# A new order for all operations of an attention and token-mixing kernel

## The chip, the cores and the metric

The kernel runs on one core of a Trainium2 chip. The metric is the device time of one launch in microseconds (us). A change of the order of operations is looked at, in a kernel whose order is written out by hand.

## The reference

For 8 batches and 8 heads, with q, k, v of 576 rows of 64 and p of 32 rows of 64:

```python
def sm_attn(qq, kk, vv):
    s = scale * np.matmul(qq, kk.transpose(0, 1, 3, 2))
    a = softmax(s)
    return np.matmul(a, vv)
p_packed = sm_attn(p, k, v)                # 32 packed rows per head
x = sm_attn(q, p_packed, p_packed)         # 576 rows per head
x = x.transpose(0, 2, 1, 3).reshape(8, 576, 512)
wq, wk = x @ w_q, x @ w_k                  # 576 x 64 each
W = (1/8) * wq @ wk.T                      # 576 x 576 per batch
out = np.maximum(W @ x, 0.0) @ w_out       # 8 x 576 x 512, float32
```

Inputs and output are float32.

## The kernel before

The text SCHEDULE holds 651 entries such as `oe2@2s` or `pv@6:4`: the name of an operation, its batch, the engine that does it (v for VectorE or DVE, s for ScalarE or ACT, g for GpSimd or POOL) or a form (A, C), and behind the colon the PSUM banks that it uses. The kernel issues them one after the other, so that each engine's queue, and each queue of transfers, has its entries in list order. Between engines only data and buffers hold an instruction back. An entry that has to wait holds up all that stands behind it in its own queue, and nothing else.

One batch goes through these operations; k and q lie in three thirds t, the output in four blocks c of 128 rows and a rest (c = 4) that two batches share:

- `LK`, `LQ`, `LV` load k, q, v of a batch (line 172, issued by POOL, with the cast to bf16). `LP`, `cw`, `wo` load p, w_q with w_k, and w_out in the same queue. The k of batch 0 comes as float32 (`k_f`, SP queue) and is cast by `cA`, `cB`.
- `kt`, `qt` turn the thirds on TensorE (PE, line 306); `ke`, `qe` bring them from PSUM to SBUF.
- `s0` (327) are the scores of p and k, `nm`, `ex` (337, 343) their softmax, `xt`, `xe` turn it; `rc1`, `mk` make the divisor.
- `pv` (389) multiplies with v, `pp` (403) divides; `pt`, `pte` turn the result; `pq`, `pqe` multiply it with w_q and w_k.
- `et`, `em` (439, 456) are the scores of q; `mx`, `sb`, `x`, `sm`, `rr`, `ml` (468 to 512) their softmax; `at`, `ae` turn it.
- `wk`, `wl`, `wq`, `g`, `y` and their evictions (`wke`, `wqe`, `ge`, `ye`), with `wkx` on POOL (582), make the factors of the token mixing; `m0`, `m1`, `m2` (648, 672) mix, `r00` to `r2` are the relu.
- `o0` to `o4` (691) are the projections with w_out, `oe0` to `oe4` evict them to o_sb0 (o0, o1), o_sb1 (o2, o3) and ox (o4).
- `st0`, `st1`, `st2` (711, 707) store o_sb0, o_sb1 and ox, all on the SP queue; in the last batch `sc0` to `sc3` (714) store single blocks.
- `u` is a matmul on zeros whose result nobody reads.

Buffers: SLOTS gives the number of buffers of each tile. k_sb, v_sb and q_sb have 6; o_sb0, o_sb1 and ox have 2. An eviction to o_sb0 of batch b therefore waits until the store of batch b - 2 has read that buffer, and likewise for o_sb1. PSUM has 8 banks; an operation that writes a bank waits for the eviction that last read it.

In form A an operation on PE uses the whole 128 columns of its weights, else two halves of 64; in form C a mix is cut into twice as many matmuls of 64 columns.

Of the kernel before, what the change touches and what calls it, by code (L numbers as in the profile page):

```python
# [7 lines left out]


SCHEDULE = """  # L10
    u@0:0 u@0:0 u@0:0 u@0:0 u@0:0 u@0:0 u@0:0 u@0:0 u@0:0 tp@0:3 cA0@0v cA1@0s cB0@0s kf1@0:7
    cB1@0v kf0@0:4 kf3@0:0 kfe3@0s kf2@0:1 LP@0 kfe1@0v lp@0v LQ@0 kfe2@0s kfe0@0v u@0:2 u@0:2
    s0@0:0 tr@0:43 nm0@0 u@0:5 u@0:5 u@0:5 qt1@0:7 nm1@0 ex0@0 LV@0 ex1@0 lq0@0v LK@1 LQ@1 u@0:5
    u@0:5 xt0@0:6 qt0@0:0 LK@2 qe1@0s cw0@0 xt1@0:7 xe0@0v qt2@0:1 rc1@0 xe1@0v mk@0 qe0@0s
    u@0:5 pv@0:5 pp0@0 u@0:2 pt@0:5 u@0:2 u@0:2 u@0:2 u@0:2 u@0:2 kt2@1:6 qe2@0s cw1@0 pte@0s
    cw2@0 et@0:0 em@0:A lq1@0s kt1@1:3 kt0@1:4 mx0@0 mx1@0 ke2@1s ke1@1v u@0:7 u@0:7 u@0:7
    qt0@1:3 sb1@0 ke0@1s cw3@0 s0@1:5 x1@0 qt1@1:4 sb0@0 u@0:0 u@0:0 u@0:0 u@0:0 kt2@2:0 kt0@2:1
# [35 lines left out]
    oe2@4v r10@5s r11@5s ml2@6g em@7 o0@5:1 pq@7:2 r2@5s mx0@7 at1@6:3 ae1@6s at0@6:4 o4@5:0
    ae0@6s mx1@7 wk@6:4 sb1@7 sb0@7 wl@6 x1@7 st0@4 wq@6:3 o3@5:5 wke@6s sm1@7v wkx@6g oe4@5v
    st2@3 x0@7 rr1@7v oe0@5s g@6:4 o2@5:6 sm0@7v ge@6s ml1@7g rr0@7v y@6:0 o1@5:7 ml2@7g ml0@7v
    oe3@5s oe2@5s pqe@7s wqe@6s at0@7:2 oe1@5s at1@7:6 ye@6v st1@4 m0@6:30C m1@6:15C ae0@7v
    ae1@7s wk@7:2 r00@6s r01@6v wl@7 wke@7s wq@7:6 r11@6v wkx@7g o1@6:7 g@7:0 o0@6:4 oe1@6s
    ge@7v y@7:2 r10@6s wqe@7v oe0@6s st1@5 ye@7v o3@6:0 st0@5 oe3@6v m2@7:1 m1@7:23 r2@7s r10@7s
# [11 lines left out]
def kernel(  # L70
# [308 lines left out]
    @op  # L379
    def pv(b, on, ks):  # L380
        if len(ks) == 1:
            ks = [ks[0], ks[0] + 1]
            S_[b]["pv"] = pair(ks[0], P)
        ps = [bank(kk, [P]) for kk in ks]
        for j in range(NJ):
            for gp in range(2):
                for h2 in range(2):
                    r = slice(64 * h2, 64 * h2 + 64)
                    nc.tensor.matmul(
                        ps[h2][64 * gp:64 * gp + 64], S_[b]["e1"][r, j, 64 * gp:64 * gp + 64],  # L390
                        S_[b]["v_sb"][r, gp::2, j, :], start=(j == 0), stop=(j == NJ - 1),
                    )
# [366 lines left out]
```

## Time and profile before

| | us |
|---|---|
| median of 3 runs | 123.13 (122.69 to 127.52) |
| profiled execution | 123.27 |
| its span, first to last instruction | 121.5 |
| PE busy | 105.8 (87%) |
| DVE busy | 91.3 (75%) |
| ACT busy | 80.5 (66%) |
| POOL busy | 56.3 (46%) |
| read from and written to HBM | 30.21 MB, 9.44 MB |

The table comes from the profile's page. Busy time of PE is that of pipelined matmuls, and 33 of them are the `u` on zeros (10.6 us). In a row of a group or of the timeline stands the line, the engine, what is written and read, the count and the time; "idle before" is how long the engine had nothing to run ahead of it, and what ended that. In the chain that ended last each step is followed back to what released it. The packets of the software queue, which carries the loads, take 72.3% of the span of the 16 transfer engines, those of the hardware queue of SP, which carries the stores and k_f, 23.3%.

### The profile page before, as it was taken

The page shows a single profiled execution, that of the slowest core. Times are in us where ns is not written, and L with a number is a line of the kernel's source. Part 1 is how long each engine was busy: PE and PEld are TensorE (multiplying, and loading weights), DVE is VectorE, ACT ScalarE, POOL GpSimd, SP SyncE. Part 2 cuts the span into 40 slices and gives each one's busy share as a digit, 9 for nine tenths or more (in the row PEclk, how much of TensorE's full clock was granted, in tenths as well). Part 3 has the DMA queues.
Part 4 walks back from the last instruction along what each step waited for, and adds up shares of the span by engine and source line. Part 5 has one row for each costly group of instructions (what it writes and reads, how often), then busy time and mean ns, then how long its engine had stood idle before and what let it go on. Part 6 is the DMA issues. An engine that isn't in the chain of part 4 may idle for free.

```text
span 121.5 us, 4739 instructions
## 1 busy us (share of the span) xinstructions
PE 105.8 (87%) x2051; PEld 70.9 (58%) x2060; DVE 91.3 (75%) x155; ACT 80.5 (66%) x176; POOL 56.3 (46%) x81
## 2 busy tenths in 40 slices
PE   6865788869998999999789999999799999999940
...
DMA  3999999999999999999999999999980037263692
GB/s 61 369 183 195 200 208 207 190 207 208 206 212 204 206 210 207 289 247 250 208 255 279 259 237 273 258 199 180 309 202 5 3 147 289 90 264 155 270 347 96
DMA packets 18069, 25.47 MB, mean 210 GB/s; under 512 B 2304, under 2 KB 14592, under 8 KB 18048
## 3 DMA queue, kind: packets, MB, share of 16 engines
q0 software_dynamic: 14064, 14.49, 72.3%
q1 hardware_dynamic: 3712, 10.62, 23.3%
q8 instruction: 16, 0.26, 0.8%
...
HBM read 30.21 MB, written 9.44 MB: 326 GB/s over the span
## 4 chain that ended last, share of the span: by engine, by line
DMA 42%; PE 30%; POOL 14%; ACT 5%; issue 4%; DVE 2%; ACTq 0%; POOLq 0%; DVEq 0%
DMA v_sb<-in_v_dram 20%; PE psum L691 14%; DMA k_sb<-in_k_dram 13%; DMA q_sb<-in_q_dram 9%; PE psum L155 3%; PE psum L306 3%; POOL q_sb L172 3%; POOL part_sum L492 3%; PE psum L648 2%; ACT o_sb L162 2%; POOL a L512 2%; POOL pT_bd L198 1%; POOL v_sb L172 1%; PE psum L456 1%; POOL k_sb L172 1%
## 5 line engine op out<-in xcount | busy, mean ns | idle before, releaser
L691 PE MATMUL psum<-w_out,reluT 128*64 128x512 bf16 (+1 forms) x196 | 31.5, 380 | 0.5 <-issue 0.2
L512 POOL TENSOR_TENSOR a<-e,rr 128x512 bf16<-128x512 f32 (+1 forms) x22 | 18.2, 853 | 12.4 <-DVE rr L501 6.3
L691 PEld LDWEIGHTS <-reluT 128*64 128x64 bf16 (+1 forms) x204 | 12.7, 106 | 9.5 <-ACT reluT L162 0.7
L468 DVE TENSOR_REDUCE mx<-psum 128x36 f32<-128x1152 f32 (+2 forms) x10 | 11.0, 1114 | 5.6 <-PE psum L456 5.1
L306 PE MATMUL psum<-ident,q_sb 128*64 128x128 bf16 x288 | 12.4, 220 | 3.1 <-DMA q_sb<-in_q_dram 2.4
L343 ACT ACTIVATE e1T<-psum,nmax 128x576 bf16<-128x576 f32 x16 | 11.7, 737 | 4.8 <-DVE nmax L337 4.6
L162 ACT ACTIVATE o_sb<-psum 128x512 f32<-128x512 f32 x19 | 11.4, 598 | 5.2 <-PE psum L691 4.5
L582 POOL TENSOR_TENSOR wkx<-wk,hmask 128x256 bf16<-128x256 bf16 x8 | 5.3, 668 | 20.0 <-ACT wk L162 15.7
L162 ACT ACTIVATE reluT<-psum 128x512 bf16<-128x512 f32 x22 | 12.3, 607 | 2.7 <-PE psum L648 2.7
L306 PEld LDWEIGHTS <-q_sb 128*64 128x64 bf16 x288 | 9.8, 109 | 5.2 <-DMA q_sb<-in_q_dram 3.8
L337 DVE TENSOR_REDUCE nmax<-psum 128x2 f32<-128x1152 f32 (+1 forms) x9 | 10.9, 1222 | 1.6 <-PE psum L327 1.5
L213 PE MATMUL psum<-blank 128*64 128x512 bf16 x33 | 10.6, 439 | 1.2 <-DVE blank L193 1.2
L480 ACT ACTIVATE e<-e 128x1152 f32<-128x1152 f32 (+2 forms) x10 | 9.7, 973 | 2.5 <-DVE e L472 1.8
L472 DVE TENSOR_TENSOR e<-psum,mx 128x1152 f32<-128x1152 f32 (+2 forms) x10 | 11.0, 1113 | 0.2
L358 POOL TENSOR_TENSOR mk<-mask,rrec 128x256 f32<-128x256 f32 x8 | 5.0, 621 | 13.0 <-DVE rrec L354 13.0
L306 PE MATMUL psum<-ident,k_sb 128*64 128x128 bf16 x252 | 10.3, 220 | 0.4 <-DMA k_sb<-in_k_dram 0.3
L168 DVE COPY o_sb<-psum 128x512 f32<-128x512 f32 x13 | 8.7, 683 | 2.3 <-PE psum L691 1.5
L486 DVE TENSOR_REDUCE rs<-e 128x36 f32<-128x1152 f32 (+2 forms) x9 | 9.6, 1075 | 0.5 <-ACT e L480 0.5
L306 PEld LDWEIGHTS <-k_sb 128*64 128x64 bf16 x252 | 8.3, 110 | 2.7 <-DMA k_sb<-in_k_dram 1.3
L162 ACT ACTIVATE qT<-psum 128x384 f32<-128x384 f32 x15 | 7.4, 498 | 1.7 <-PE psum L306 1.6
L162 ACT ACTIVATE a2T<-psum 128x320 f32<-128x320 f32 (+1 forms) x12 | 4.7, 418 | 4.3 <-PE psum L155 4.0
L162 ACT ACTIVATE kT<-psum 128x384 f32<-128x384 f32 (+2 forms) x14 | 6.3, 480 | 1.4 <-PE psum L306 1.2
...
## 6 DMA issues: line engine op xcount, KB each, us to landing
out_dram<-o_sb SPq DMA_DIRECT2D x14, 512.0 KB, 5.4
q_sb<-in_q_dram POOLq DMA_DIRECT2D x8, 576.0 KB, 13.2
v_sb<-in_v_dram POOLq DMA_DIRECT2D x8, 576.0 KB, 12.3
k_sb<-in_k_dram POOLq DMA_DIRECT2D x7, 576.0 KB, 16.3
k_f<-in_k_dram SPq DMA_DIRECT2D x2, 576.0 KB, 4.8
out_dram<-ox SPq DMA_DIRECT2D x4, 256.0 KB, 4.6
out_dram<-o_sb SPq DMA_DIRECT2D x4, 256.0 KB, 3.1
w_out<-in_moe_w_out_dram POOLq DMA_DIRECT2D x2, 256.0 KB, 9.7
```

Source lines behind the costliest of these rows:

```text
L162: nc.scalar.activation(dst, src, func, scale=scale)
L168: nc.vector.tensor_copy(dst, src)
L213: nc.tensor.matmul(bank(ks[0], [n])[0:64], blank[:, 0:64], blank[:, 0:n], start=True, stop=True)
L306: nc.tensor.transpose(ps[64 * g2:64 * g2 + 64, 2 * gp:2 * gp + 2, jj, :], S_[b][src][:, gp + 2 * g2, j], ident,)
L337: nc.vector.tensor_reduce(tile("nmax", [P, 2], fp32, b)[:, h], S_[b]["s1"][:, h], axis=AX, op=MAX, negate=True)
L343: nc.scalar.activation(tile("e1T", [P, NJ, 2, 64], bf16, b)[:, :, h2], S_[b]["s1"][:, h2].rearrange("a (j s) -> a j s", s=64), EXP, bias=S ...
L468: nc.vector.tensor_reduce(tile("mx", [P, NU, 1], fp32, b)[:, r], S_[b]["e"][:, r], axis=AX, op=MAX)
L472: nc.vector.tensor_tensor(tile("e2", [P, NU, L], fp32, b)[:, r], S_[b]["e"][:, r], S_[b]["mx"][:, r].to_broadcast((P, r.stop - r.start, L) ...
L480: nc.scalar.activation(e, e, EXP, scale=scale)
L486: nc.vector.tensor_reduce(dst, src, axis=AX, op=ADD)
L512: (nc.vector if on == "v" else nc.gpsimd).tensor_tensor(tile("a2", [P, NU, L], bf16, b)[:, r], S_[b]["e2"][:, r], S_[b]["rr"][:, r].to_bro ...
L691: nc.tensor.matmul(ps[r], src[:, h2, gp, o + r.start:o + r.stop], w_out[:, 2 * gp + h2, :], start=(h2 + gp == 0), stop=(h2 + gp == 2),)
```

## The change

The list is written anew: 655 entries in place of 651. Every operation of the old list is in the new one, and four `u` are added. The order differs nearly everywhere, some entries name another engine, another bank or another form, and `pv` can take a form E, which no entry uses. SLOTS and all else are the same. Of the list the rows that hold the loads and the stores of the first half, and the entries around them, are shown:

```diff
 SCHEDULE = """
-    u@0:0 u@0:0 u@0:0 u@0:0 u@0:0 u@0:0 u@0:0 u@0:0 u@0:0 tp@0:3 cA0@0v cA1@0s cB0@0s kf1@0:7
-    cB1@0v kf0@0:4 kf3@0:0 kfe3@0s kf2@0:1 LP@0 kfe1@0v lp@0v LQ@0 kfe2@0s kfe0@0v u@0:2 u@0:2
-    s0@0:0 tr@0:43 nm0@0 u@0:5 u@0:5 u@0:5 qt1@0:7 nm1@0 ex0@0 LV@0 ex1@0 lq0@0v LK@1 LQ@1 u@0:5
-    ...
-    LV@1 qe1@1s nm0@1 qt2@1:4 x0@0 ex1@1 sm0@0v kt1@2:2 LK@3 LQ@2 sm1@0v ex0@1 xt0@1:5 pq@0:7
-    ke2@2s rr0@0v ke0@2s wo1@0 ke1@2s rr1@0v xt1@1:0A ml1@0v ml0@0g ml2@0g qe2@1v pqe@0v at1@0:4
-    wo0@0 xe0@1s xe1@1v rc1@1 s0@2:5 LV@2 mk@1 at0@0:2 ae1@0s pv@1:0 ae0@0s LK@4 nm0@2 pp0@1
-    ...
-    o0@0:0A rr0@1v LQ@5 qe1@2s mk@2 LV@4 r11@0s nm0@3 ml0@1g ml1@1g ex1@3 r10@0v pv@2:2 o3@0:7A
-    ...
-    m1@1:70C pt@3:6A nm0@4 o1@1:5A qe2@3v pte@3s at1@2:6A LQ@6 ex0@4 r10@1v r11@1v o4@1:1A
-    ...
-    oe2@1s kt2@5:5 ge@2s ke0@5v sm0@3v y@2:0 rr0@3v pv@4:2 ye@2s m0@2:01C st0@0 pp0@4 r00@2v
-    ...
-    et@4:0 oe3@1s at1@3:5A st1@0 ml0@3g em@4:A qe2@5s o2@2:3A ae1@3s at0@3:5A oe2@2s o1@2:7A
-    mx0@4 ae0@3v wk@3:5A wl@3 wq@3:3 kt2@6:4 sb0@4 wqe@3v qt0@5:6 oe1@2s s0@5:0 pq@4:3 wke@3s
-    kt0@6:5 x0@4 qe0@5v pqe@4s ke2@6s nm0@5 qt1@5:6 wkx@3g kt1@6:7 ke0@6s sm0@4g ke1@6v st0@1
-    ...
-    xt1@5:7A rc1@5 oe0@2v kt2@7:5 rr0@4v r00@3s mk@5 ml1@4g xe0@5v kt0@7:6 r01@3s s0@6:0 xe1@5s
-    ...
-    ex1@6 pte@5s ml0@4g LV@6 st2@1 et@5:0 LQ@7 ml2@4g st1@1 ke1@7v oe2@3v o3@3:4A em@5:A qe2@6s
-    ...
-    o0@3:3A LV@7 r2@3s sb0@5 wl@4 rc1@6 mk@6 qt1@6:5 xe1@6s s0@7:0 wq@4:4 wke@4v oe0@3s wkx@4g
-    x0@5 nm0@7 pv@6:6 wqe@4s qe1@6s pp0@6 g@4:3A ge@4v o4@3:4A ex0@7 sm0@5v y@4:5 qt0@6:3
-    ...
-    ge@5s qe0@7v st0@2 y@5:0 pv@7:3 ye@5s st1@3 sm0@6v m0@5:67C pp0@7 m1@5:01C oe1@4s pq@6:5
-    ...
+    LP@0 LK@1 LQ@0 cA1@0s u@0:0 u@0:0 u@0:0 u@0:0 u@0:0 u@0:0 u@0:0 u@0:0 u@0:0 tp@0:0 LV@0 LK@2
+    cB0@0v cB1@0v LQ@1 cA0@0v u@0:1 u@0:1 u@0:1 u@0:1 u@0:1 u@0:1 u@0:1 kf3@0:4 cw3@0 kf0@0:5
+    kfe3@0v LV@1 lp@0v kf2@0:1 kfe0@0s kf1@0:4 kfe2@0s tr@0:26 kfe1@0v cw0@0 s0@0:3 nm0@0 ex0@0
+    ...
+    LK@3 pp0@0 pt@0:0A nm0@1 pte@0s u@0:2 et@0:0 em@0:A mx0@0 ex1@1 kt1@2:3 mx1@0 kt2@2:4 ex0@1
+    ...
+    u@0:0 at0@0:4 qe1@1v s0@2:0 ml2@0v LV@2 pv@1:5 ae0@0v pq@0:4 pp0@1 LK@4 at1@0:3A nm0@2
+    pt@1:5A wo1@0 pte@1s pqe@0s u@0:7 et@1:5 ae1@0s em@1:A wo0@0 ex0@2 wk@0:3A mx0@1 wl@0 wke@0s
+    ...
+    r01@0s u@0:2 pv@2:1 r11@0v ml2@1g qe0@2s ml0@1g qe2@2s s0@3:4 pp0@2 nm0@3 LV@4 u@0:3 at0@1:1
+    ...
+    sb0@3 qe0@4s wl@2 qt2@4:0 wke@2s kt2@5:7 pqe@3v kt1@5:6 wkx@2g x0@3 qe2@4v m0@1:12C LV@5
+    ...
+    qt0@5:3 pte@4v kt0@5:1 qe0@5s et@4:4 em@4:A ke0@5v qe1@5s oe2@1s at0@3:3A mx0@4 at1@3:0A
+    ae0@3s st1@1 m1@2:27C ae1@3s m0@2:13C r10@2s st0@0 o1@1:0A r11@2s sb0@4 r00@2s wk@3:2A
+    oe1@1s wl@3 wq@3:7 r01@2v x0@4 s0@5:4 wke@3v qt2@5:1 nm0@5 kt1@6:3 wqe@3s wkx@3g kt0@6:0
+    qe2@5s kt2@6:2 LQ@6 ke0@6s pq@4:7 kt2@7:1 ke1@6v ex0@5 kt1@7:0 LV@6 pqe@4v g@3:3A sm0@4v
+    ...
+    oe1@2s m1@3:34 LQ@7 xe1@5v s0@6:0 xe0@5v r10@3s o0@2:7 LV@7 r11@3s nm0@6 ml2@4g pv@5:3
+    oe0@2s ml0@4g m0@3:65 ex0@6 pp0@5 st0@2 kt0@7:7 pt@5:3 ml1@4g st2@1 ex1@6 o2@2:4 pte@5v
+    ke0@7v st1@0 r00@3s et@5:1 st0@1 qt0@6:0 r01@3s em@5:A qe0@6s xt1@6:5A mx0@5 xt0@6:6A xe1@6s
+    o3@2:0A xe0@6s at0@4:5A rc1@6 oe2@2s oe3@2v mk@6 qt2@6:6 o3@3:7 ae0@4s sb0@5 qe2@6s pv@6:4
+    ...
+    m2@3:4A sm0@5v wk@4:7A o2@3:3A ex1@7 r2@3s et@6:0 em@6 rr0@5v oe1@3s rc1@7 ml0@5g qt2@7:4
+    ...
+    pv@7:3 ye@4s rr0@6v ae0@5s m0@4:12 oe4@3s ml0@6g pp0@7 m1@4:75 wq@5:0 r01@4s st2@3 pt@7:3
+    ...
+    oe1@7s o2@7:0A sc1@7 oe0@7v o3@7:5A sc0@7 oe2@7v o4@7:4A sc2@7 oe3@7s sc3@7 oe4@7s st2@7
 """
 ...
@@ -107,8 +107,8 @@
     for item in SCHEDULE.split():
         name, rest = item.split("@")
         b, ks = rest.split(":") if ":" in rest else (rest, "")
-        on = ks[-1] if ks[-1:] in ("A", "C") else b[-1] if b[-1] in "vsg" else ""
-        items.append((name, int(b.rstrip("vsg")), on, [int(x) for x in ks.rstrip("AC")]))
+        on = ks[-1] if ks[-1:] in ("A", "C", "E") else b[-1] if b[-1] in "vsg" else ""
+        items.append((name, int(b.rstrip("vsg")), on, [int(x) for x in ks.rstrip("ACE")]))
     listed = {(name, b): on for name, b, on, _ in items}
 
     sbp = ctx.enter_context(tc.tile_pool(name="sbp", bufs=1))
@@ -381,6 +381,18 @@
         if len(ks) == 1:
             ks = [ks[0], ks[0] + 1]
             S_[b]["pv"] = pair(ks[0], P)
+        if on == "E":
+            ps = [bank(kk, [Dh]) for kk in ks]
+            S_[b]["pv"] = pair(ks[0], Dh).unsqueeze(2).to_broadcast((P, 2, 2, Dh))
+            for j in range(NJ):
+                for u in range(4):
+                    for h2 in range(2):
+                        r, c = slice(64 * h2, 64 * h2 + 64), slice(32 * u, 32 * u + 32)
+                        nc.tensor.matmul(
+                            ps[h2][c], S_[b]["e1"][r, j, c], S_[b]["v_sb"][r, u // 2 + 2 * (u % 2), j, :],
+                            start=(j == 0), stop=(j == NJ - 1),
+                        )
+            return
         ps = [bank(kk, [P]) for kk in ks]
         for j in range(NJ):
             for gp in range(2):
@@ -400,7 +412,10 @@
                 mask.rearrange("r g d -> r (g d)"), op0=MULT, op1=MULT,
             )
         else:
-            nc.vector.tensor_tensor(t, S_[b]["pv"], S_[b]["mk"], op=MULT)
+            m = S_[b]["mk"]
+            if len(S_[b]["pv"].shape) == 4:
+                t, m = (x.rearrange("r h (g d) -> r h g d", g=2) for x in (t, m))
+            nc.vector.tensor_tensor(t, S_[b]["pv"], m, op=MULT)
 
     for i in range(2):
         ops[f"pp{i}"] = lambda b, on, ks, i=i: pp(i, b)
```

More of the change, by code (lines that the diff above doesn't have):

```diff
@@ L53 @@
[L53 to L58, printed above, removed]
@@ L59 @@
-    m0@7:64 r00@7v st0@6 o2@6:5 r11@7s o3@7:1 oe2@6s r01@7v o4@7:5 o2@7:0 o0@7:3 st2@5 o1@7:4
-    st1@6 oe3@7v sc3@7 oe4@7s st2@7 oe2@7v oe0@7v sc2@7 oe1@7s sc0@7 sc1@7
+    LP@0 LK@1 LQ@0 cA1@0s u@0:0 u@0:0 u@0:0 u@0:0 u@0:0 u@0:0 u@0:0 u@0:0 u@0:0 tp@0:0 LV@0 LK@2
+    cB0@0v cB1@0v LQ@1 cA0@0v u@0:1 u@0:1 u@0:1 u@0:1 u@0:1 u@0:1 u@0:1 kf3@0:4 cw3@0 kf0@0:5
+    kfe3@0v LV@1 lp@0v kf2@0:1 kfe0@0s kf1@0:4 kfe2@0s tr@0:26 kfe1@0v cw0@0 s0@0:3 nm0@0 ex0@0
+    u@0:7 u@0:7 u@0:7 u@0:7 u@0:7 kt1@1:1 nm1@0 ex1@0 rc1@0 u@0:7 u@0:7 u@0:7 u@0:7 u@0:7
@@ new lines @@
+    pt@1:5A wo1@0 pte@1s pqe@0s u@0:7 et@1:5 ae1@0s em@1:A wo0@0 ex0@2 wk@0:3A mx0@1 wl@0 wke@0s
+    u@0:4 kt1@3:4 ex1@2 wkx@0g kt2@3:3 sb0@1 LQ@3 ke2@3s g@0:0 xt1@2:1A LV@3 ke1@3v xt0@2:2A
+    x0@1 wq@0:3 xe0@2v LQ@4 pq@1:5 rc1@2 xe1@2v qt0@2:4 ge@0s wqe@0s sm0@1v mk@2 y@0:6 qt2@2:0
+    ye@0s LK@5 kt0@3:3 pqe@1s qt1@2:1 ke0@3s rr0@1v m0@0:56C qe1@2v m1@0:37 ml1@1g r00@0s r10@0v
+    r01@0s u@0:2 pv@2:1 r11@0v ml2@1g qe0@2s ml0@1g qe2@2s s0@3:4 pp0@2 nm0@3 LV@4 u@0:3 at0@1:1
+    pt@2:2A ae0@1s at1@1:3A pte@2s ae1@1v et@2:0 ex1@3 em@2:A wk@1:3A LQ@5 ex0@3 mx0@2 wl@1
@@ new lines @@
+    wq@1:7 wke@1s kt1@4:4 pq@2:5 wkx@1g rc1@3 kt2@4:6 sb0@2 ke1@4s xt0@3:3 wqe@1s LK@6 o1@0:4A
+    xe0@3s LK@7 pqe@2v x0@2 xt1@3:0A g@1:5A mk@3 kt0@4:2 ge@1v xe1@3s o2@0:1 sm0@2v oe1@0s
+    ke0@4s qt1@3:4 ke2@4s y@1:2 qe1@3s rr0@2v s0@4:5 ye@1v ml0@2g qt2@3:4 nm0@4 o3@0:0 qe2@3s
+    ml2@2g qt0@3:4 ml1@2g oe3@0v ex1@4 pv@3:2 oe2@0s o0@0:0A pp0@3 ex0@4 at0@2:1A m2@1:2A qe0@3s
+    at1@2:3A oe0@0s r2@1v pt@3:5A xt0@4:4A ae0@2s pte@3v m1@1:67C ae1@2s rc1@4 qt1@4:0 r10@1s
+    mk@4 et@3:1 pq@3:5 qe1@4s em@3:A xe0@4s o4@1:0A r11@1s mx0@3 wk@2:6A oe4@1s qt0@4:7 wq@2:4
```

45 lines of the change are left out of this document (20 added, 25 removed).

## The prediction

> **What bounds the kernel now.** I read the page first, then the matrix engine's and the SP queue's timelines, the chain that ended last, and each transfer's time to landing.
>
> ```profile
> span 121.5 us, 4739 instructions
> PE 105.8 (87%) x2051; PEld 70.9 (58%) x2060; DVE 91.3 (75%) x155; ACT 80.5 (66%) x176; POOL 56.3 (46%) x81
> PE   6865788869998999999789999999799999999940
> DMA  3999999999999999999999999999980037263692
> ```
>
> The slices are 3.04 us long. Transfers fill the first 30 (91 us): the loads stream without a pause. PE is near full from slice 9 on. So two things run side by side, a load stream that ends at 91 us and a PE row that is dense from about 27 us to 117 us. PE's timeline shows how rarely loads still stop it late on, and the chain shows how it ends:
>
> ```profile
> 39.89 0.70 PE L389 MATMUL psum<-v_sb,e 64*64 64x128 bf16 x36
> 61.24 0.70 PE L389 MATMUL psum<-v_sb,e 64*64 64x128 bf16 x36 [1.26 <-DMA v_sb<-in_v_dram]
> 83.88 0.70 PE L389 MATMUL psum<-v_sb,e 64*64 64x128 bf16 x36
> 87.25 0.53 PE L306 MATMUL psum<-ident,q_sb 128*64 128x128 bf16 x12 [0.78 <-DMA q_sb<-in_q_dram]
> ...
> 111.32 5.33 PE psum L691 x48
> 116.66 0.02 issue
> ```
>
> L389 is operation pv: these are pv@2, pv@4 and pv@6. After pv@2 only pv@4 (1.26 us) and qt1@7 (0.78 us) wait for a load. From pv@2 to the last projection PE takes 116.66 - 39.89 = 76.8 us; from there to the end of the span lie 121.5 - 116.7 = 4.8 us (last eviction, last store). Outside the span lie 123.27 - 121.5 = 1.77 us of the profiled execution, which is 0.14 us above the median of the runs.
>
> **The change, part by part.** It adds a form of pv (letter E) that no entry of the new list uses: nothing. The list keeps every operation, adds four dummy matmuls u, and reorders the rest.
>
> **1. Loads.** The two w_out loads stood ahead of v_sb of batch 2 (v2); now they stand behind k4.
>
> ```profile
> 21.23 0.74 POOL L172 DMA_DIRECT2D q_sb<-in_q_dram  x1 [2.09 <-DMA q_sb<-in_q_dram]
> 27.77 0.76 POOL L172 DMA_DIRECT2D v_sb<-in_v_dram  x1
> 29.10 0.80 POOL L172 DMA_DIRECT2D k_sb<-in_k_dram  x1
> ...
> q_sb<-in_q_dram POOLq DMA_DIRECT2D x1, 576.0 KB, 12.1
> v_sb<-in_v_dram POOLq DMA_DIRECT2D x1, 576.0 KB, 10.9
> k_sb<-in_k_dram POOLq DMA_DIRECT2D x1, 576.0 KB, 12.4
> ```
>
> The last three rows are issue to landing of the three issues above. q2 lands at 33.3, v2 at 38.7, k4 at 41.5: 2.8 us for a load, 5.4 us where the w_out loads lie between, so w_out costs 2.6 us and v2 lands at 36.1. The k load of batch 1 now goes ahead of q0 and v0, which come one load (2.8 us) later; v1 keeps its place, and pv@1 waits for it in both lists, so I carry nothing of that beyond pv@1. pv@2 can start between 36.1 (the load alone) and 42.7 (39.9 plus the 2.8 not made good); its other inputs, evictions on ACT and DVE, come about 1 us after the load in my count: 37.2. Late on, v5 is issued behind wkx@2 and q6 behind wkx@3; the queue then still holds k6, k7 and v5, which cover that (2.8 us each; without them the stream would pause by that much).
>
> **2. PE's work.** Prices, from the chain:
>
> ```profile
> 27.89 0.51 PE psum L327 x6
> ...
> 87.78 0.54 PE psum L648 x8
> 92.15 0.48 PE psum L592 x4
> 92.63 0.34 PE psum L306 x12
> 95.20 0.50 PE psum L389 x36
> 102.93 0.88 PE psum L691 x8
> 110.76 0.56 PE psum L648 x16
> ```
>
> A projection (o, L691) is 0.88, a third of a transpose (kt, qt, L306) 0.34, wq (L592) 0.48, the scores s0 (L327) 0.51. A mix in form C (L648) is 0.54; the sixteen at 110.76 are two mixes without C, 0.28 each. Six mixes lose their C: 6 x 0.26 = 1.6 us less. Projections and transposes that change between halves and whole matmuls I take at no change. The four u add at most 0.9 us ahead of pv@2, where PE waits for loads anyway. Behind pv@2 the new list has o0@0 and o1@0 more (1.8), s0@3 (0.5), one u (0.2), and all six cheaper mixes (1.6): 0.9 us more than before. v4 and q7 land earlier without stores in between, so I drop 1.26 + 0.78 = 2.0 us of waits. PE without any new wait: 37.2 + 76.8 + 0.9 - 2.0 = 112.9 (111.8 from the lower bound, 118.4 from the upper).
>
> **3. ACT and DVE.** 142 evictions on ACT for 132, 66 on DVE for 76, and the sum sm0@4 goes from POOL to DVE. By the rows of each form that is 5.4 us more on ACT and 6.6 us less on DVE.
>
> ```profile
> 36.00:48.00 12.00, 11.51 (x227) 7.79 (x225) 10.41 (x17) 9.50 (x22) 7.67 (x11) 1.00 1.21 207
> 60.00:75.00 15.00, 13.65 (x271) 9.39 (x274) 12.07 (x21) 11.44 (x25) 8.47 (x12) 1.00 1.16 250
> ```
>
> Columns: PE, PEld, DVE, ACT, POOL. ACT is idle for 2.5 of 12 us and 3.6 of 15 us there, and PE for less; the added work fits in ACT's idle time: nothing. If that cover is gone, up to 5.4 us come onto PE.
>
> **4. Stores, the part that decides.** All stores but none of the loads go through SP, in list order. The old order is st0@0, st1@0, st0@1, st2@1, st1@1, st1@2, st0@2. The new one is st1@1, st0@0, st0@2, st2@1, st1@0, st0@1. A list place does not hold a store back, but what stands ahead of it does: st0@0 and st1@0, whose data are ready by about 50 us, now stand behind st1@1 (data from oe2@1) and behind st0@2 (data from oe0@2). o_sb0 and o_sb1 have two buffers each. oe1@2 overwrites what st0@0 reads; oe2@2 (ACT) and oe3@2 (DVE) overwrite what st1@0 reads. Such waits cost almost nothing before (the tile's list of idle time), and what a store takes is in the SP timeline and the landings:
>
> ```profile
>   DMA out_dram<-o_sb: 0.2, 1
> ...
> 58.80 0.54 SPq L711 DMA_DIRECT2D out_dram<-o_sb  x1
> 59.38 0.59 SPq L707 DMA_DIRECT2D out_dram<-ox  x1
> 73.18 1.19 SPq L711 DMA_DIRECT2D out_dram<-o_sb  x2
> 80.17 3.31 SPq L711 DMA_DIRECT2D out_dram<-o_sb  x2
> ...
> out_dram<-o_sb SPq DMA_DIRECT2D x1, 512.0 KB, 7.7
> out_dram<-o_sb SPq DMA_DIRECT2D x1, 512.0 KB, 6.9
> out_dram<-ox SPq DMA_DIRECT2D x1, 256.0 KB, 7.8
> out_dram<-o_sb SPq DMA_DIRECT2D x1, 512.0 KB, 5.1
> out_dram<-o_sb SPq DMA_DIRECT2D x2, 512.0 KB, 5.4
> out_dram<-o_sb SPq DMA_DIRECT2D x1, 512.0 KB, 8.1
> out_dram<-o_sb SPq DMA_DIRECT2D x1, 512.0 KB, 7.9
> out_dram<-o_sb SPq DMA_DIRECT2D x1, 512.0 KB, 4.0
> ```
>
> The landings belong to the issues at 44.85, 58.80, 59.38, 73.18, the pair 73.18 and 73.82 (median), 80.17, 82.94 and 97.93. With loads queued a store needs 6.9 to 8.1 us; near 73 us, with the load queue almost empty, 5.1; after the loads 4.0. A follower adds little when the queue is empty (73.82 + 5.7 = 79.5, 1.2 us behind the first) and 1.5 us for half the size when loads stream (65.7 and 67.2), so 2.6 to 3 for 512 KB.
>
> *First wait.* Counted back from the end by part 2's prices, o0@2 starts at about 70.2 without waits: it starts at 70.33 in the old trace, from where 46.3 us follow; the new list has 2.8 less (kt1@7, kt2@7, s0@6, m1@3, xt@5, y@3 are done earlier, five C mixes cheaper, o2@2 more) and 0.8 of load wait less: 42.7. Between oe2@1 and o0@2 stand 8.5 us of PE work (two projections 1.8, six thirds 2.0, three mixes 1.4, two s0 1.0, smaller ones 2.3), so oe2@1 starts at about 61.4, and st1@1 goes at 62.1, st0@0 at 62.7. oe1@2 is due at 69.1, 6.4 us later. st0@0 needs between 5.6 (empty queue) and 9.3 (6.9 to 7.7 for the first, less the 0.6 between the issues, plus 2.6); I take 8.0, as loads stream: a stall of 1.6 us (0 to 2.9). o0@2 uses bank 7, which oe1@2 clears, so PE waits too: o0@2 at 71.4.
>
> *Second wait.* oe0@2 ends at 71.4 + 0.88 + 0.6 = 72.9. SP then issues st0@2 at 73.0, st2@1 at 73.6, st1@0 at 74.2. With the empty-queue price st1@0 lands at 73.0 + 5.1 + 0.6 + 1.2 = 79.9; with the streaming price at 73.0 + 7.7 + 1.3 + 2.6 = 84.6. From k4 (41.5 less the 2.6 of w_out, which follow it) ten loads of 2.8 us and the 3 us of two stores put q6's landing at 72.5, so v6, q7 and v7 are still to come at 73 us: I take 83.0, near the latter. oe2@2 wants to start some 4.5 us after oe0@2. Behind it on ACT stand ae0@4 and all later evictions, behind oe3@2 on DVE sb0@5; pv@6 needs banks 4 and 5, which oe2@2 and ae0@4 clear:
>
> ```profile
> L162 ACT ACTIVATE o_sb<-psum 128x512 f32<-128x512 f32 x19 | 11.4, 598 | 5.2 <-PE psum L691 4.5
> L162 ACT ACTIVATE a2T<-psum 128x320 f32<-128x320 f32 (+1 forms) x12 | 4.7, 418 | 4.3 <-PE psum L155 4.0
> ```
>
> So pv@6 starts at 83.0 + 0.6 + 0.4 + 0.1 = 84.1. Without the wait it would start at 77.5 (below).
>
> *From pv@6 to the end.* 116.66 - 83.88 = 32.8 us in the old trace. The new list has more behind it: o0@3, o1@3, o2@3 (2.6), s0@7, wq@4 (1.0), at1@4, wk@4, wl@4, m2@3 (0.9), less four C mixes (1.0) and q7's wait (0.8): 35.4 us (77.5 + 35.4 = 112.9 again). After a stop of that length the other engines have caught up, so I add nothing.
>
> **Sum.** 84.1 + 35.4 = 119.5 for PE, + 4.8 = 124.3 span, + 1.8 = 126.1, and 126.0 against the median. Bounds: no first wait and the empty-queue price put st1@0 at 78.7, 4.3 us less: 121.7. The full first wait (1.3 more) and the streaming price (1.6 more) give 128.9.
>
> Two rules of the Trainium skill bear on this part. DMA: Bandwidth & Descriptors (Anatomy of one DMA) fits a transfer as about 2.0 us plus its bytes over 436 GB/s, for the software queue; a 512 KB store would be an estimated 3.2 us. The rows after the loads (4.0) are near it, those within the stream (6.9 to 8.1) are not, so the measured ones stand; by the rule the time would be the first rival's. TensorE: Matmul & The Clock Gate (Part 1) says that the array falls to half clock after some 3.4 us of idleness and needs as long to come back. PE's clock column is 1.00 in the rows above and its longest late wait 1.26 us, so no run here shows it; the stall forecast would then cost an estimated 1.7 us more, 127.7.
>
> **Rivals.**
> *A, the stores are home in time (faster).* If a store takes the 4.0 us of the row after the loads, and followers 0.6 and 1.2, st0@0 lands before 69.1 and st1@0 at 71.8 + 4.0 + 1.8 = 77.6, when oe2@2 is due at about 76 and PE has 1.2 us of other work: PE ends at 112.9, the time is 112.9 + 4.8 + 1.8 = 119.5. It decides if st1@0 lands less than about 5 us after its issue. For it: the row at 97.93. Against it: five rows of 6.9 us and more among loads.
> *B, waits at the empty-queue price.* 121.7 to 125; for it the 5.1 us at 73.18, the very time of the burst; against it, that dip was there because v6 had not been issued, while the new list issues q6 to v7 by about 72.
> *C, the loads take the place of the stores.* The burst is 1.8 MB ahead of and between v6, q7 and v7. At a follower's 1.2 us for 512 KB v7 lands at 72.5 + 8.4 + 4.2 = 85, at 2.6 us near 90. Behind pv@7 (95.20 in the chain) the old trace has 21.5 us, the new list three projections (2.6) and smaller work (0.9) more: PE ends at 113 to 115, the time is 119.5 to 121.6. It counts only where A holds.
> *D, no effect.* The same operations on an almost full PE: 123.1. For it PE's dense row; against it the counts of parts 2 and 4, which would have to cancel.
>
> **How the numbers follow.** Forecast (both waits, near streaming price) 0.60; B 0.17; A with C 0.17; D 0.06. A change of less than 2% (120.7 to 125.6 us) could hardly be told from none here. B, D and a tenth of the forecast fall within it (0.17 + 0.06 less the little of B above it, with part of the low forecast: 0.23), A and C below it (0.19 with B's low edge), the rest above: 0.58. The forecast's own range is 121.7 to 128.9; to leave no more than 2 in 10 out, the range takes in C and the edge of A: 120.8 to 129.2.
>
> **What would show it.** Right: SP issues st1@1 first, near 62 us; idle time of ACT and DVE put down to out_dram<-o_sb of 3 us or more in all, at oe1@2 and oe2@2; a PE gap ahead of pv@6 that ends at 82 to 86 us; pv@2 near 37; 35 to 36 us from pv@6 to PE's last projection. Wrong: these tiles wait under 1 us for stores, or pv@6 starts before 79 us (then A or C), or PE's gaps lie ahead of pv@2, or are put down to ACT all along (then part 1 or 3 failed).

## The result and the profile after

The changed kernel takes 131.0 us (median of 4, 130.19 to 132.04) against 123.19 us of the kernel before beside it: ratio 1.0654, 95% interval 1.0552 to 1.0755. It is slower by 6.5%, where 126.0 us were forecast. (Medians here are over all runs of a kernel; the ratios leave out runs that were clearly slower than the fastest of the same kernel.) The profiled execution took 130.78 us. Its page:

```profile
span 128.9 us, 4654 instructions
PE 109.4 (85%) x2014; PEld 72.4 (56%) x2026; DVE 87.2 (68%) x147; ACT 82.6 (64%) x185; POOL 53.9 (42%) x76
PE   6869798799889999999999993059999999999930
PEclk9999999999999999999999999955999999999998
DMA  3999999999999999999999999980007704607891
```

A slice is now 3.22 us. PE's row is full from slice 12 on, and then has a hole in slices 24 to 26 (from 77 us on) that the old row has not. Behind the hole the clock row falls to 5 for two slices. The list of waits names what made the hole (total, times, longest, in us):

```profile
ACT o_sb L162 <- DMA out_dram<-o_sb: 7.9, 1, 7.9
DVE o_sb L168 <- DMA out_dram<-o_sb: 7.3, 1, 7.3
PE psum L401 <- ACT o_sb L162: 6.6, 1, 6.6
```

One wait of ACT, one of DVE, both on a store, and one of PE (L401 is pv) on ACT. SP's timeline shows which store. The first row is st1@1, st0@0 and, at its end, st0@2; then st2@1; the last row begins with st1@0:

```profile
62.75 10.70 SPq L726 DMA_DIRECT2D out_dram<-o_sb  x3
73.48 0.59 SPq L722 DMA_DIRECT2D out_dram<-ox  x1
74.12 24.34 SPq L726 DMA_DIRECT2D out_dram<-o_sb  x5
```

The chain that ended last runs through that very store (10.27 us to landing), the eviction oe2@2 and pv@6:

```profile
74.12 10.27 DMA out_dram<-o_sb
84.47 0.61 ACT o_sb L162
85.12 0.26 PE psum L401
```

On PE's timeline pv@2, pv@4 and pv@6 answer to the rows of before:

```profile
36.62 0.70 PE L401 MATMUL psum<-v_sb,e 64*64 64x128 bf16 x36
...
58.88 0.67 PE L401 MATMUL psum<-v_sb,e 64*64 64x128 bf16 x36
...
85.12 1.44 PE L401 MATMUL psum<-v_sb,e 64*64 64x128 bf16 x36 [6.58 <-ACT o_sb L162]
...
122.68 1.03 PE L706 MATMUL psum<-w_out,reluX 128*128 128x512 bf16 x4
```

Up to pv@4 the changed kernel is 2.4 us ahead of the old one (61.24), at pv@6 1.2 us behind (83.88), and PE ends at 123.7 us for 116.66. pv@6 has also a longer duration, 1.44 us for 0.70, while the clock is down. The windows behind the hole (columns PE, PEld, DVE, ACT, POOL, granted clock, DMA share, GB/s):

```profile
76.00:85.00 9.00, 2.49 (x30) 1.38 (x29) 1.66 (x3) 1.14 (x4) 0.61 (x1) 0.91 1.11 283
85.00:88.00 3.00, 2.87 (x56) 2.13 (x55) 2.19 (x4) 2.38 (x5) 0.00 (x0) 0.50 0.54 112
88.00:91.00 3.00, 2.78 (x29) 1.89 (x27) 2.97 (x4) 2.01 (x7) 0.00 (x0) 0.64 0.02 5
91.00:94.00 3.00, 3.00 (x89) 2.15 (x87) 1.59 (x3) 2.51 (x7) 2.63 (x4) 1.00 0.00 0
```

PE has work in nearly all of 85 to 91 us, but at a granted clock of 0.50 and 0.64. The theory to be tested was therefore: the whole loss is the place of st1@0 in SP's order, paid as a wait and then as a lower clock. The rival: the new order as such (loads, engines, work on PE) costs something too.

### The profile page after: what moved, and what is told of

The parts are those of the page before. It is cut to its first block, busy times and chain, and to the rows that moved or that the text cites. A ratio compares the mean times of both kernels' runs of the same rounds, so it can differ in the third digit from the quotient of the medians.

```text
span 128.9 us, 4654 instructions
## 1 busy us (share of the span) xinstructions
PE 109.4 (85%) x2014; PEld 72.4 (56%) x2026; DVE 87.2 (68%) x147; ACT 82.6 (64%) x185; POOL 53.9 (42%) x76
## 4 chain that ended last, share of the span: by engine, by line
PE 56%; DMA 15%; DVE 13%; ACT 7%; issue 3%; POOL 1%; SPq 1%; DVEq 0%; ACTq 0%; POOLq 0%
PE psum L706 17%; DMA out_dram<-o_sb 10%; PE psum L306 9%; PE psum L155 7%; DMA k_f<-in_k_dram 5%; PE psum L401 4%; PE psum L327 4%; PE psum L663 3%; DVE mx L483 3%; DVE e L487 3%; PE psum L471 3%; DVE nmax L337 2%; PE psum L607 2%; ACT e L495 2%; ACT e1T L343 1%
## 5 line engine op out<-in xcount | busy, mean ns | idle before, releaser
L527 POOL TENSOR_TENSOR a<-e,rr 128x512 bf16<-128x512 f32 (+1 forms) x22 | 18.7, 870 | 26.3 <-DVE rrec L354 13.4
L706 PEld LDWEIGHTS <-reluT 128*64 128x64 bf16 (+1 forms) x172 | 12.1, 105 | 10.6 <-issue 1.7
L162 ACT ACTIVATE reluT<-psum 128x512 bf16<-128x512 f32 x27 | 15.0, 607 | 0.6 <-PE psum L663 0.5
L213 PE MATMUL psum<-blank 128*64 128x512 bf16 x37 | 12.0, 440 | 1.2 <-DVE blank L193 1.2
L401 PE MATMUL psum<-v_sb,e 64*64 64x128 bf16 x288 | 6.3, 229 | 6.6 <-ACT o_sb L162 6.6
L501 DVE TENSOR_REDUCE rs<-e 128x36 f32<-128x1152 f32 (+2 forms) x10 | 11.1, 1110 | 0.7 <-ACT e L495 0.5
L162 ACT ACTIVATE qT<-psum 128x384 f32<-128x384 f32 x20 | 9.4, 500 | 3.3 <-PE psum L306 3.2
L162 ACT ACTIVATE kT<-psum 128x384 f32<-128x384 f32 (+1 forms) x18 | 8.2, 493 | 4.5 <-PE psum L262 3.5
L306 PE MATMUL psum<-ident,k_sb 128*64 128x128 bf16 x252 | 10.8, 221 | 0.1
L401 PEld LDWEIGHTS <-e 64*64 64x64 bf16 x288 | 5.0, 114 | 8.5 <-issue 8.0
## 6 DMA issues: line engine op xcount, KB each, us to landing
q_sb<-in_q_dram POOLq DMA_DIRECT2D x8, 576.0 KB, 12.5
```

The source lines that it names most:

```text
L162: nc.scalar.activation(dst, src, func, scale=scale)
L213: nc.tensor.matmul(bank(ks[0], [n])[0:64], blank[:, 0:64], blank[:, 0:n], start=True, stop=True)
L306: nc.tensor.transpose(ps[64 * g2:64 * g2 + 64, 2 * gp:2 * gp + 2, jj, :], S_[b][src][:, gp + 2 * g2, j], ident,)
L401: nc.tensor.matmul(ps[h2][64 * gp:64 * gp + 64], S_[b]["e1"][r, j, 64 * gp:64 * gp + 64], S_[b]["v_sb"][r, gp::2, j, :], start=(j == 0), s ...
L501: nc.vector.tensor_reduce(dst, src, axis=AX, op=ADD)
L527: (nc.vector if on == "v" else nc.gpsimd).tensor_tensor(tile("a2", [P, NU, L], bf16, b)[:, r], S_[b]["e2"][:, r], S_[b]["rr"][:, r].to_bro ...
```

## Experiments

**The store alone, in the new list.** The changed kernel with st1@0 right behind st0@0, ahead of st0@2 and st2@1:

```diff
-... st1@1 m1@2:27C ... r10@2s st0@0 o1@1:0A ... st0@2 ... st2@1 ex1@6 ... ke0@7v st1@0 r00@3s ...
+... st1@1 m1@2:27C ... r10@2s st0@0 st1@0 o1@1:0A ... st0@2 ... st2@1 ex1@6 ... ke0@7v r00@3s ...
```

> The new list with one entry moved: st1@0 stands right behind st0@0, so ahead of st0@2. Theory 1 (oe2@2 and oe3@2 wait for a store that is queued behind st0@2): st1@0 is issued near 64 us, the waits of the two o_sb tiles for stores fall from 15.2 us in all to under 1 us, pv@6 starts at 78.5 us (the end of o3@3 in the changed kernel) in place of 85.1, the clock stays at 1.00, and the time is 131.0 - 6.6 - 2.6 = 121.8 us, 120.5 to 123. Theory 2 (the rest of the order costs time by itself, the store only shows it): another wait fills the place, pv@6 or a later step is as late, over 126 us.

Measured: 123.1 us, ratio to the kernel before 0.9996 (0.9944 to 1.0047). Page, then oe2@2 on ACT's timeline and pv@6 on PE's:

```profile
span 120.9 us, 4666 instructions
PE   6998789689988999999999999998999999999940
```

```profile
77.20 0.59 ACT L160 ACTIVATE o_sb<-psum 128x512 f32<-128x512 f32 x1
...
79.20 0.70 PE L399 MATMUL psum<-v_sb,e 64*64 64x128 bf16 x36
```

The hole is gone, oe2@2 starts without a wait at 77.20, and pv@6 at 79.20 us. So one store's place carries the whole loss of 6.5%. What is left of the change is worth nothing: it gains 3.2 us up to pv@2 (36.65) and loses all but 0.5 us of it until PE's end (116.2 for 116.66). The windows from pv@2 to PE's end, first of the kernel before, then of this one, say where:

```profile
39.89:116.66 76.77, 73.94 (x1465) 49.94 (x1472) 63.50 (x103) 56.77 (x125) 30.57 (x43) 1.00 0.90 214
```

```profile
36.65:116.20 79.55, 77.80 (x1459) 51.31 (x1458) 60.99 (x95) 63.02 (x141) 30.34 (x41) 1.00 0.91 215
```

PE is idle for 2.83 us before and 1.75 us now, but busy for 3.9 us more. (Nine matmul records of some 2060 are missing in the old trace, so such shares hold to a few tenths of a us; the lengths of the windows do not depend on them.)

**The store alone, in the old list.** The converse: the kernel before, with st1@1 right behind oe3@1 and st1@0 behind it.

```diff
-... oe3@1s at1@3:5A st1@0 ml0@3g ...  ml2@4g st1@1 ke1@7v ...
+... oe3@1s st1@1 st1@0 at1@3:5A ml0@3g ...  ml2@4g ke1@7v ...
```

> The old list with two entries moved: st1@1 right behind oe3@1 and st1@0 right behind st1@1, so that the store of batch 0's o_sb1 is queued behind data that are ready at about 64.7 us, and nothing else. Theory 1 (a store held back in SP's queue, a buffer that waits for it, then PE): st1@0 goes at 65.4 us and lands 7.5 to 9.5 us later, near 74; oe2@2, due at 66.7 us, waits about 7 us; PE stops behind it for 5 to 7 us, and the clock falls to one half for some 5 us (2.6 us more): 130 to 133 us. If the delay of a store only matters in the new list: 123 us.

Measured: 131.5 us, ratio 1.0641 (1.048 to 1.0801). ACT's and PE's timelines, then the windows:

```profile
72.84 1.08 ACT L160 ACTIVATE o_sb<-psum 128x512 f32<-128x512 f32 x2 [9.10 <-DMA out_dram<-o_sb]
```

```profile
73.49 1.07 PE L590 MATMUL psum<-a2T,pqk 128*64 128x512 bf16 x4 [7.79 <-ACT o_sb L160]
```

```profile
66.00:74.00 8.00, 0.51 (x4) 0.31 (x5) 0.26 (x1) 1.16 (x3) 0.00 (x0) 0.68 1.10 307
74.00:78.00 4.00, 4.00 (x64) 3.46 (x62) 2.42 (x3) 2.31 (x5) 3.08 (x4) 0.50 0.22 49
78.00:82.00 4.00, 4.00 (x52) 2.25 (x48) 2.83 (x8) 2.23 (x6) 1.47 (x4) 0.85 0.01 4
```

Two stores moved in the old list, with nothing else changed, give the time of the whole change, by the same wait, the same hole and the same low clock.

**The wait without the low clock.** The changed kernel, with 28 dummy matmuls in the hole:

```diff
-... mk@6 qt2@6:6 o3@3:7 ae0@4s ...
+... mk@6 qt2@6:6 u@0:7 (28 times) o3@3:7 ae0@4s ...
```

> The new list with 28 dummy matmuls u (6.0 us) ahead of o3@3, in the time in which PE has nothing to do. The wait for the store stays: pv@6 near 85 us. Theory (the half clock behind the stall costs time of its own): the granted clock stays at 1.00 from 85 to 91 us, pv@6 takes 0.7 us in place of 1.4, and the time is 131.0 - 2.6 = 128.4 us (127.5 to 129.5). If the slow start behind the stall is only the refilling of the other engines: 131 us, unchanged.

Measured: 128.38 us, ratio 1.0476 (1.0395 to 1.0558). Waits, PE's timeline, windows:

```profile
ACT o_sb L162 <- DMA out_dram<-o_sb: 8.5, 2, 8.0
```

```profile
77.52 5.78 PE L213 MATMUL psum<-blank 128*64 128x512 bf16 x26
...
85.22 0.97 PE L401 MATMUL psum<-v_sb,e 64*64 64x128 bf16 x36 [0.63 <-ACT o_sb L162]
...
121.10 1.03 PE L706 MATMUL psum<-w_out,reluX 128*128 128x512 bf16 x4
```

```profile
85.00:88.00 3.00, 2.62 (x65) 1.89 (x65) 2.77 (x4) 2.64 (x6) 0.00 (x0) 1.00 0.39 77
88.00:91.00 3.00, 2.92 (x65) 1.94 (x65) 2.63 (x6) 2.87 (x9) 0.21 (x1) 1.00 0.02 5
```

The store is as late as before (8.0 us) and pv@6 starts as late (85.22), but the clock stays at 1.00 and the time falls by 2.6 us (by the ratios, 1.0654 and 1.0476, it is 2.2). More work made the kernel faster. Between pv@6 and PE's end it is 122.1 - 85.2 = 36.9 us here, for 123.7 - 85.1 = 38.6 in the changed kernel: these 1.7 us of the loss of 7.8 are the clock's. The other 0.9 lie behind PE's end (126.4 - 122.1 = 4.3 us for 128.9 - 123.7 = 5.2), and nothing here shows that the clock made them. Some 5.2 us are left for the wait. All four runs bear the clock out: their mean granted clock is 0.992 to 1.00 with the dummies, 0.958 to 0.969 without.

**More buffers instead.** The changed kernel with four buffers for o_sb1, and mk on two to make room.

```diff
-... mk=3 ... o_sb1=2 ...
+... mk=2 ... o_sb1=4 ...
```

> The new list as it is, with 4 buffers for o_sb1 in place of 2 (and 2 for mk in place of 3, to make room). The stores keep their order, so st1@0 lands at about 84 us as before, but oe2@2 and oe3@2 write another buffer. Theory 1 (reuse of the buffer is the wait): no wait there, pv@6 at 78.5 us, clock 1.00, 121.8 us (120.5 to 123). If instead the late store itself (its place in the transfer queues) held up the kernel, pv@6 stays near 85 us and the time near 131 us.

Measured: 127.77 us, ratio 1.0413 (1.0348 to 1.0478). oe2@2 no longer waits and pv@6 starts at 79.68 us. But ACT's and PE's timelines have a new wait, at oe1@3, which overwrites what st0@1 reads; that store stands last in the same burst, and o_sb0 still has two buffers:

```profile
88.80 1.08 ACT L160 ACTIVATE o_sb<-psum 128x512 f32<-128x512 f32 x2 [4.28 <-DMA out_dram<-o_sb]
```

```profile
89.45 1.06 PE L605 MATMUL psum<-a2T,pqk 128*64 128x512 bf16 x4 [4.27 <-ACT o_sb L160]
```

The granted clock in 88 to 91 us is 0.62. The burst has two late stores, and with the first out of the way the second one decides.

**All early stores as soon as their data are there.**

```diff
 order of the stores on SP
-st1@1 st0@0 st0@2 st2@1 st1@0 st0@1
+st1@0 st0@0 st2@1 st1@1 st0@1 st0@2
```

> The new list with the first six stores (st1@0, st0@0, st2@1, st1@1, st0@1, st0@2) each right behind the evictions they need. Theory 1: no waits of o_sb tiles for stores, as when st1@0 alone is moved; but five stores now run within the load stream before 66 us, where 512 KB cost the stream about 1.5 us, so PE waits for a load once or twice between 58 and 75 us (1 to 2 us): 122 to 124 us. Theory 2: over 126 us. If early stores cost the stream nothing, 121.5 us as with the one entry moved.

Measured: 124.31 us, ratio 1.0124 (1.0036 to 1.0212). No eviction waits for a store. The loads pay instead, by PE's timeline:

```profile
61.88 0.53 PE L304 MATMUL psum<-ident,q_sb 128*64 128x128 bf16 x12 [1.46 <-DMA q_sb<-in_q_dram]
...
80.59 0.70 PE L399 MATMUL psum<-v_sb,e 64*64 64x128 bf16 x36 [0.32 <-DMA v_sb<-in_v_dram]
```

So there is a gain in stores that begin late while loads stream: the loads behind them come sooner. It is worth only some 1.3% here (1.0124 against 0.9996 with st1@0 alone ahead, two intervals that just overlap), and the new list bought it at 6.5%.

**The w_out loads.** The kernel with st1@0 ahead, and wo1@0, wo0@0 back in front of LV@2.

```diff
-... LV@2 pv@1:5 ... wo1@0 pte@1s ... wo0@0 ex0@2 ...
+... wo1@0 wo0@0 LV@2 pv@1:5 ... pte@1s ... ex0@2 ...
```

> The new list with st1@0 behind st0@0 and the two w_out loads ahead of v2 in the load queue, as the old list has them. Theory A (v2's landing sets pv@2, the step of the prediction): v2 lands 2.6 us later, pv@2 starts near 38.9 in place of 36.6 us, and PE, dense behind it, ends 1.5 to 2.3 us later: 124.5 to 125.5 us. Theory B (pv@2's time is not what sets the end, later waits absorb it): 123 us.

Measured: 124.96 us, ratio 1.0119 (1.007 to 1.0168). PE's timeline has pv@2 wait for v2:

```profile
38.02 0.70 PE L399 MATMUL psum<-v_sb,e 64*64 64x128 bf16 x36 [1.54 <-DMA v_sb<-in_v_dram]
```

pv@2 is 1.4 us later than 36.65, and the time 1.9 us longer than 123.1 (1.5 by the ratios). To load w_out behind v2 is a part of the change that pays. It is not all of the 3.2 us that pv@2 comes earlier: in the old list PE does two projections from 38.06 to 39.89 us, right ahead of pv@2, which the new list does later.

**Mixes without C.** The kernel before with all 13 C mixes in the plain form.

```diff
-m0@0:01C ... m1@1:70C ... m0@4:01C ...
+m0@0:01 ... m1@1:70 ... m0@4:01 ...
```

> The old list with all 13 mixes of form C written without C. By the chain's rows a mix falls from 0.54 to 0.28 us: 13 x 0.26 = 3.4 us less PE work, 12 of them behind pv@2. Theory A (PE's work sets the end): 120 to 121 us. Theory B (evictions and loads set it, PE's spare time is spread as small waits): 122.5 to 123.2 us.

Measured: 124.75 us, median of 4 (122.62 to 125.5), the kernel before 122.97 beside it; no interval. Nothing of the 3 us is seen: the shortest run, 122.62 us, is no shorter than the shortest of the kernel before, 122.43. The times say no more than that, but the traces do. PE's timeline has the same two entries, m0@2 and m1@2, with C in the kernel before (first fence) and without (second); under each stands that kernel's group of all mixes:

```profile
61.87 0.61 PE L648 MATMUL psum<-wqT,y 64*128 64x256 bf16 x8
```

```profile
L648 PE MATMUL psum<-wqT,y 64*128 64x256 bf16 (+1 forms) x76 | 5.3, 274 | 0.0
```

```profile
61.55 0.63 PE L646 MATMUL psum<-wqT,y 64*64 64x256 bf16 x16
```

```profile
L646 PE MATMUL psum<-wqT,y 64*64 64x256 bf16 x128 | 5.4, 276 | 0.0
```

A pair of mixes takes 0.6 us in either form, and all of them 5.3 or 5.4 us. The fences also set right what was said of form C ahead of the prediction: C does not double the matmuls of a mix but halves them. A mix with C is 4 matmuls on all 128 columns of the weights, as in form A, and one without is 8 on 64 columns each (13 x 4 + 3 x 8 = 76, and 16 x 8 = 128). By that description eight matmuls are one mix with C, and the prediction took a piece of eight, 0.54 us, for one, where it is two.

**The old list's engines.** The kernel with st1@0 ahead, and the engine letter of 95 entries as in the old list.

```diff
-... qe1@1v ... ml2@0v ... ae0@0v ... r11@0v ... pqe@3v ...
+... qe1@1s ... ml2@0g ... ae0@0s ... r11@0s ... pqe@3s ...
```

> The new list with st1@0 behind st0@0, and every eviction and DVE or POOL step on the engine that the old list names for it (95 entries change their letter, no order changes). Theory A (the ten more evictions on ACT cost PE its small waits): 120.5 to 122 us, PE's idle time behind pv@2 falls from 6.7 to about 4.5 us. Theory B (letters and order were planned together, DVE is as much in the way as ACT): no gain, 123 to 126 us.

Measured: 133.65 us, ratio 1.0852 (1.0771 to 1.0933). Windows of this kernel, then of the one with the new letters:

```profile
38.00:60.00 22.00, 16.97 (x343) 12.34 (x343) 16.93 (x27) 12.26 (x29) 8.60 (x12) 1.00 1.22 208
```

```profile
38.00:60.00 22.00, 21.63 (x435) 15.27 (x432) 17.28 (x27) 17.96 (x41) 9.93 (x14) 1.00 1.22 208
```

PE is idle for 5.0 of 22 us with the old letters, in pieces of about 1 us that mostly wait for DVE; with the new ones it is idle for 0.4. ACT's 5.7 us more and PE's 4.7 us more of busy time go together: the letters belong to the order, and neither can be judged alone.

**Towards a faster kernel: the old list with quieter stores.** st1@2 and st0@2 behind st1@3, so that no store starts between 73 and 82 us; and, in the second kernel, st1@0, st2@1, st0@0 behind oe4@1 as well.

```diff
 order of the stores on SP
-st0@0 st1@0 st0@1 st2@1 st1@1 st1@2 st0@2 st1@3 st0@3
+st0@0 st1@0 st0@1 st2@1 st1@1 st1@3 st1@2 st0@2 st0@3
```

> Old list with two stores moved: st1@2 and st0@2 go behind st1@3, so that no store starts between about 73 and 82 us, while the last loads (q7, v7) land. Theory A (each store started within the load stream delays the loads behind it by some 1.5 us): q7 lands 1 to 2 us earlier, PE's wait of 0.78 us for it at qt1@7 goes, the three stores then stand in one burst near 82 us, whose data buffers (o_sb0 of batch 2, o_sb1 of batches 2 and 3) are needed again by oe1@4 and oe2@4 only near 95 us; 122.3 us, ratio 0.993. Theory B (the loads are bound by their own stream and PE's wait for q7 is covered by other work, or the burst makes oe0@4 or oe2@4 wait): 123.1 us or up to 125, with idle time of ACT put down to out_dram<-o_sb.

> The edit of e10 and, in addition, st1@0, st2@1 and st0@0 moved behind oe4@1 (near 54 us), so that the store at 44.85 us no longer stands within the loads ahead of v4. Theory A: v4 lands 1 to 1.5 us earlier, PE's 1.26 us wait at pv@4 goes, and the later operations move by as much: 121.5 us, ratio 0.986. Risk that both theories share: oe1@2 (near 68 us) waits if st0@0 lands later than that, and then 123 us or more. Theory B (waits for loads are covered): 123.1 us, as e10.

Measured: 122.8 us, ratio 0.9892 (0.9819 to 0.9966), and 125.1 us, ratio 1.0096 (1.0036 to 1.0155), the kernel before at 124.0. The second kernel's wait at pv@4 grew to 2.58 us: three stores now fall into the 10 us ahead of v4's landing, which I had not counted. The first kernel's profile is of an execution of 124.62 us, longer than its median; what was long in it lies ahead of the edit. PE's timeline at pv@4, and windows of 2 us behind it:

```profile
62.02 0.70 PE L387 MATMUL psum<-v_sb,e 64*64 64x128 bf16 x36 [1.81 <-DMA v_sb<-in_v_dram]
```

```profile
60.00:62.00 2.00, 0.21 (x6) 0.09 (x5) 1.10 (x2) 0.77 (x2) 0.34 (x1) 1.00 1.24 215
62.00:64.00 2.00, 1.98 (x60) 1.66 (x61) 1.14 (x3) 0.60 (x1) 2.00 (x3) 0.81 1.12 270
64.00:66.00 2.00, 2.00 (x19) 0.96 (x14) 0.48 (x1) 1.17 (x4) 0.07 (x1) 0.50 1.11 302
```

pv@4 starts 0.8 us later than in the old trace, and the clock fell to 0.50 behind a wait of 1.81 us. (In the second kernel's trace it is at 0.50 from 64 to 66 us too, behind the 2.58 us.) Two more kernels put five dummy matmuls ahead of pv@4, with and without the moved stores:

```diff
-... y@2:0 rr0@3v pv@4:2 ye@2s ...
+... y@2:0 rr0@3v u@0:2 u@0:2 u@0:2 u@0:2 u@0:2 pv@4:2 ye@2s ...
```

> The edit of the kernel that moves st1@2 and st0@2 behind st1@3, and five dummy matmuls u (0.22 us each, 1.1 us together by the row of 26 in 5.78 us) right ahead of pv@4, where PE waits 1.26 to 2.6 us for v4. Theory A (the granted clock falls after an idle stretch between 1.26 and 1.81 us, as the profiles of the two kernels with quieter stores show: 1.81 us idle, then 0.67 over 64 to 68 us): clock 1.00 from 60 to 72 us whenever v4 is up to 2.5 us late, the highest times go, median 122.0 us, ratio 0.983, and pv@4 to PE's end takes about 55 us. Theory B (the clock dip is not caused by the idle time, or its 1.3 us are covered by the load stream's pace): as without the five, ratio 0.989.

> The old list with the five dummy matmuls ahead of pv@4 and nothing else. Theory A: the idle stretch in front of pv@4 shrinks from 1.3 to 1.8 us to 0.2 to 0.7, the clock stays at 1.00 behind it, median 0.5 to 1 us below the old list's on the same chip, ratio 0.994. Theory B: no change, ratio 1.000; up to 1.005 if v4 is on time and the five stand in its way.

Measured: 122.61 us, ratio 0.9981 (0.9937 to 1.0026), and 123.86 us, ratio 1.0008 (0.9948 to 1.0068), the kernel before at 123.79. PE's timeline of the first:

```profile
60.55 1.27 PE L211 MATMUL psum<-blank 128*64 128x512 bf16 x5
...
62.42 0.70 PE L387 MATMUL psum<-v_sb,e 64*64 64x128 bf16 x36 [0.60 <-DMA v_sb<-in_v_dram]
```

Here v4 is even later, and the clock is at 1.00 over all of 56 to 80 us; from pv@4 to PE's end it is 117.0 - 62.4 = 54.6 us, where the execution without the five needed 118.2 - 62.0 = 56.2 (both ends by the last projections in their chains). The wait for q7 is in neither trace. So two single executions, taken on two chips, differ by 1.6 us where the clock differs, and the wait for q7 is about 0.8 us (116.66 - 61.24 = 55.4 in the old trace, less 54.6). That the five matmuls kept the clock up is not shown: in the same two traces PE waits 1.84 and 2.18 us for q_sb, up to 12.5 and 12.8 us, and the clock stays at 1.00 there without any help. In the times both come to no more than the interval: 0.989 was not repeated by the kernel with the same edit, and no kernel here is shown to beat the old one.

## Why the prediction was right in its direction and wrong in its size

- **Part 1, loads: right.** v2 was forecast to land at 36.1 and landed at 27.4 + 8.0 = 35.4; pv@2 was forecast at 37.2 and started at 36.62. The w_out experiment puts 1.4 us of pv@2's start on that move, and 1.5 to 1.9 us of the time.
- **Part 2, PE's work: wrong, by 3 us of work and 1 us of waits.** It had 0.9 us more work from pv@2 on and 2.0 us less waiting. With the store out of the way the windows show 3.9 us more work and 1.1 us less waiting. Of the 3.0 us, 1.6 are the mixes without C, a misread price: they cost what those with C cost. The other 1.4 no run attributes, and some tenths of them may be records that the old trace lacks. Without the wait the change gives 123.1 us, not the 119.5 of rival A.
- **Part 3, ACT and DVE: right, with its reason too weak.** The added work on ACT costs nothing, and taken back it costs 10 us: it relieves DVE, for which PE then waits.
- **Part 4, first wait: no stall.** st1@1 went at 62.75, 0.6 us behind the count. st0@0 landed near 70.3 us, close to the 70.7 counted, but ACT had other work until 70.50 us, 1.4 us longer than counted, and so oe1@2 found its buffer free: the list of waits has a single wait of ACT for a store, that of oe2@2. That oe0@2 ended where forecast, at 72.9, is luck: the text got there with a wait that did not occur.
- **Part 4, second wait: right, 1 us short.** Place, releaser and victims are those of the text. st1@0 landed at 84.4, not 83.0; the text's full streaming price had 84.6. pv@6 started at 85.1, not 84.1. The 10.27 us are three times the estimated 3.2 us which the Trainium skill's fit gives (DMA: Bandwidth & Descriptors, Anatomy of one DMA); of that rule the trace bears out nothing while loads stream.
- **From pv@6 to PE's end: the step that failed.** 38.6 us instead of 35.4. With the clock held at 1.00 it is 36.9 us, and without the hole 116.2 - 79.2 = 37.0: 1.6 us are the mis-sizing of part 2. Its share here is work, 36.2 us busy of these 37.0 for 31.8 of 32.8 in the old trace, so 4.4 us more where 3.5 were counted (1.0 was taken off for four C mixes); and waits, 0.8 us idle for 1.0, where the whole 0.8 of q7's wait was taken off. The other 1.7 us are the clock: "After a stop of that length the other engines have caught up, so I add nothing" was wrong, as PE itself came back at half clock. The Trainium skill (TensorE: Matmul & The Clock Gate, Part 1) says that an idle array falls to half clock, and the text priced it at an estimated 1.7 us but left it out since no row showed it. By that rule 127.7 would have been forecast. The trace agrees that the clock falls to half (0.50 behind 6.58 us), and the estimate of 1.7 us is what was measured; as the clock stayed low for longer than the rule's 3.4 us (0.64 still over 88 to 91 us), that match is in part luck.
- **Sum.** 1.0 (pv@6) + 1.6 (work and waits) + 1.7 (clock) + 0.4 (tail, 5.2 for 4.8) are the 4.7 us between 126.1 and the profiled 130.78. All four have one sign, so the range missed too.
- **Rivals.** A, B and C did not occur: st1@0 needed 10.27 us, far from the 4.0 of A and the 5.1 of B. D describes the change without its store.
